# Every third weight remainder of three expert slots made by GpSimd instead of VectorE

## The chip, the cores and the metric

The kernel runs on one core of a Trainium2 chip. The core's engines run side by side, each through its own list of instructions in order: TensorE (PE in the profile; PEld is its loading of weights), VectorE (DVE), ScalarE (ACT), GpSimd (POOL) and SyncE (SP). Semaphores hold an instruction back until what it needs is done. The metric is the device time of one execution in microseconds; of several runs, the median.

## The reference

Attention comes first, then a layer of experts that takes the attention's output as its rows (3584 tokens of 768 values):

```python
q_n, k_n = (rmsnorm(q, g_q), rmsnorm(k, g_k))     # 8 batches, 12 heads, 448 positions, 64 values
scores = scale * np.matmul(q_n, k_n.transpose(0, 1, 3, 2))
attn = softmax(scores); x = attn @ v               # put together to x: 3584 x 768
logits = x @ w_gate + modality_bias[modality_id]   # 8 experts
e_idx = np.argmax(logits, axis=1)                  # one expert for each token
for e in range(8):
    h = np.maximum(x[mask] @ w1[e], 0.0)           # 768 -> 1024
    out[mask] = gate_w[mask, None] * (h @ w2[e])   # 1024 -> 768
```

All of it is in float32. The change touches only how `w1` is made ready for the product `x[mask] @ w1[e]`.

## The kernel before, in words

**Three products for one.** TensorE works here on a rounded 32-bit type (fp32r). To keep accuracy, a matrix is split into a rounded part and a remainder: `high = round(w)`, `low = w - high`. The product is then the sum of three, high times high, high times low and low times high. The first layer's weights are split by `split1`: ScalarE casts a piece of the raw weights `r1` into `w1h`, and VectorE subtracts it from the raw piece and writes the remainder to `w1l`. Both lie in the tile `w1w`. A piece is 128 partitions by 256 values; a slot needs 24 of them (4 groups `jj` of hidden values by 6 chunks `i` of the 768 inputs). The raw weights lie so that the 256 values of a piece are every eighth value of a row (`"p (c m j) -> p c j m"` with `j=8`), 32 bytes apart.

**Slots.** The tokens are sorted by expert into blocks of 256 rows, and a slot is one block. Fourteen slots run in a fixed loop (`for s in range(NSTAT)`), and what is left of the data goes through a tail behind it. A slot has two halves:

- the first layer (`mm1_half`, L485): eight beats, each 18 matmuls, two beats for each `jj`. The sums lie in two PSUM buffers `ph`, which ScalarE and VectorE empty into `hhw` and `hlw`; VectorE and ScalarE also split the second layer's weights here (`split2`, into `w2ha`/`w2hb` and `w2lw`);
- the second layer (`mm2_step`, L515): sixteen beats `b_`. Here the next slot is made ready: its rows are transposed after beats 9, 11 and 13 (`xtr`, L468, tile `px`), and split by ScalarE and VectorE into `xw`; and its 24 pieces of weights are split, two a beat in beats 0 to 11, by the loop `while s + 1 < NSTAT and k_ < ...`. The order of the pieces is chunks 0 to 2 of each of the four `jj`, then chunks 3 to 5 of each.

**The order is written out by hand.** `tc.manual_schedule` covers all five engines: every engine runs its instructions in the order in which the Python code issues them, and only the waits are added. So a place in the loop is a place in each engine's list. Most small operations go through the class `Deferred`, whose line 52 issues them at once (L52 in the profile) and whose line 53 issues those that were collected in a list and are dealt out later, five a beat (`little`).

**GpSimd's list.** In the slots before the change, GpSimd only issues indirect DMAs: `wload` (weights of a coming slot into `r`, which is `r1`, in beat 13, and into `r2w` during the first layer; a block of the same expert as the one before skips the rows but not the instruction), `xload` (rows of the slot after next into `xrw`, in beat 12, and for slot 3 at the start of slot 2; from slot 3 on two gathers for each half of the rows, the second of which waits for the first to land), the output scatter `out_dram<-yw` after each half of the second layer, `route_put` (`l_d<-lt`, the sorted token lists, in slots 0 and 1) and the gathers of the lists `lt<-l_d`. Six of the latter stand in slot 1 behind beat 10's pieces; VectorE works them up (`lb_x2f`, `lb_x2i`, `lb_oi`, `lb_o`) behind beat 15.

**Slots 0 and 1 differ from the others.** In slot 0, VectorE also finishes the routing of the last batch (`route_mm`, `route_pos`; tiles `rtc`, `bs`, `pf`), and in slot 1 it works out the tables of the remaining slots (`tables2`; tiles `tb_...`).

Of the kernel before, what the change touches and what calls it, by code (L numbers as in the profile page):

```python
# [9 lines left out]
F32 = mybir.dt.float32  # L10
# [3 lines left out]
ALU = mybir.AluOpType  # L14
# [43 lines left out]
def deferred(fn):  # L58

    Deferred.queue = items = []  # L60
    fn()
    Deferred.queue = None
    return items
# [3 lines left out]
def kernel(  # L67
# [15 lines left out]
    V, A, G = (Deferred(e, n) for e, n in ((nc.vector, "op"), (nc.scalar, "act"), (nc.gpsimd, "dma")))  # L83
    PE, SY = nc.tensor, nc.sync
    GP = Deferred(nc.gpsimd, "op")
# [16 lines left out]
        out=tri, in_=ones[:CP, :CP], pattern=[[1, CP]], compare_op=ALU.is_gt,  # L102
# [249 lines left out]
    def view(t, off, p, *dims):  # L352
        n = 1
        for d in dims:
            n *= d
        a = t[:p, off : off + n]
        if len(dims) > 1:
            ax = " ".join("abcd"[: len(dims)])
            a = a.rearrange(f"p ({ax}) -> p {ax}", **dict(zip("abcd"[1:], dims[1:])))
        return a  # L360
# [43 lines left out]
    w1h, w1l = ([view(w1w, 1536 * (2 * j + o), 128, 6, 2, 128) for j in range(4)] for o in range(2))  # L404
# [22 lines left out]
    def wload(s, which, halves=(0, 1)):  # L427
        tb, i = tb_of(s)
        raw, src = ((r1, w1v), (r2, w2v))[which]
        for h in halves:  # L430
            G.indirect_dma_start(out=raw[h], out_offset=None, in_=src,
                                 in_offset=IOFF(ap=tb["wi"][:, i, h : h + 1], axis=0),
                                 bounds_check=NE * 256 - 1, oob_is_err=False)

    def split1(jj, n0=0, n1=6):
        for i in range(n0, n1):
            h, c = divmod(i, 3)
            rs = r1[h].rearrange("p (c m j) -> p c j m", c=3, j=8)[:, c, 2 * jj : 2 * jj + 2]
            A.copy(w1h[jj][:, i], rs)
            V.tensor_tensor(out=w1l[jj][:, i], in0=rs, in1=w1h[jj][:, i].bitcast(F32), op=ALU.subtract)  # L440

    def split2(jj, only=None):
        rs = r2[jj // 2].rearrange("p (c f) -> p c f", c=4)[:, 2 * (jj % 2) : 2 * (jj % 2) + 2]
# [5 lines left out]
    def xload(s):  # L449
        tb, i = tb_of(s)  # L450
        xr = []
        for t in range(2):
            x = xr_b[s % 2][t]
            G.indirect_dma_start(out=x, out_offset=None, in_=x1_d[:],
                                 in_offset=IOFF(ap=lt2[:, s, t, 0:1].bitcast(I32), axis=0),
                                 bounds_check=NT1 - 1, oob_is_err=False)
            if tb["x2i"] is not None:
                G.indirect_dma_start(out=x, out_offset=None, in_=x2_d[:],
                                     in_offset=IOFF(ap=tb["x2i"][:, i, t : t + 1], axis=0),
                                     bounds_check=NT - NT1 - 1, oob_is_err=False)  # L460
            xr.append(x.rearrange("p (m c) -> p c m", c=6))
        return xr
# [14 lines left out]
    def mm1_open(s, jj):  # L477
        return ps_s.tile([128, 2, TB], F32, tag="s", name=f"ph{s}_{jj}")
# [27 lines left out]
    def mm2_open(s, t):  # L506
        pools = ((ps_t, "t"), (ps_t, "t")) if t == 0 else ((ps_m, "m"), (ps_o, "o"))
        return [p.tile([128, 512], F32, tag=tg, name=f"py{s}_{t}{n}") for n, (p, tg) in enumerate(pools)]
# [179 lines left out]
    if True:  # L688
# [354 lines left out]
        def route_mm(b, pool=(ps_t, "t")):  # L1043
            oh = RT[b]["oh"]
            ps = pool[0].tile([128, 512], F32, tag=pool[1], name=f"rt{b}")
            ohf = oh.rearrange("p c e -> p (c e)")
            PE.matmul(ps[:, 0:32], lhsT=ones[:CP, :128], rhs=ohf, start=True, stop=True)
            PE.matmul(ps[:CP, 32:64], lhsT=tri, rhs=ohf, start=True, stop=True)
            pc = rp.tile([128, 2, NCH, NE], F32, tag="rtc", name=f"rtc{b}")
            RT[b]["pc"] = pc  # L1050

            def evac():
                for i, r in ((0, slice(0, 128)), (1, slice(0, CP))):
                    V.tensor_copy(out=pc[r, i].rearrange("p c e -> p (c e)"), in_=ps[r, 32 * i : 32 * i + 32])

            return evac
# [32 lines left out]
        def route_put(b, c):  # L1089
            posi, lt = RT[b]["posi"], RT[b]["lt"]  # L1090
            G.indirect_dma_start(out=l_d[:], out_offset=IOFF(ap=posi[:, c : c + 1], axis=0),
                                 in_=lt[:, c, :], in_offset=None)
# [59 lines left out]
        def at(where, n, fn):  # L1152
            where.setdefault(n, []).append(fn)

        def run(where, n):
            for f in where.pop(n, ()):
                f()
# [29 lines left out]
        for u in range(NU):  # L1187
            for j in range(NJ):
                jj = (0, 1, 2, 4, 5, 6, 3)[j] if u < P["early"] else j
# [24 lines left out]
        for n in range(P["start"], NJ * NU):  # L1214
            i, j = divmod(n, NJ)
# [105 lines left out]
        def go(*fs):  # L1321

            for f in fs:
                r = f() or ()
                for g in after:
                    g()
                after[:] = r if isinstance(r, (list, tuple)) else [r]

        def part(fn, *a):
            return lambda: fn(*a)  # L1330
# [41 lines left out]
        def little(m):  # L1372
            for _ in range(min(m, len(small))):
                small.pop(0)[1]()

        for s in range(NSTAT):

            beat = {}
            if s > 0:
                if s == 1:  # L1380
                    xr = xn
                    for c in range(2):
                        at(beat, 3 * c, lambda c=c: route_put(B - 1, 2 + c))
                if s > 1:
                    xr = xn
                if s == 2:
                    xr = []
                    at(beat, 1, lambda: xr.extend(xload(3)))
                for b_ in range(4):
                    at(beat, 2 * b_, part(split2, b_))  # L1390
                    if b_ % 2:
                        at(beat, 2 * b_, part(wload, s + 1, 1, (b_ // 2,)))
                if s == 1:
                    small += deferred(tables2)
                elif s < NS2 - NS1:
                    for kind, fn in deferred(lambda: state["get2"](s + 1, 1 if s < NSTAT - 1 else NS2 - NSTAT)):
                        at(beat, 3 if kind == "dma" else 16, fn)
                for b_ in range(8):
                    if b_ % 2 == 0:
                        p0 = mm1_open(s, b_ // 2)  # L1400
                    go(part(mm1_half, s, b_ // 2, b_ % 2, p0))
                    run(beat, b_)
                    little(5)
            else:
                for c in range(NCH):
                    at(beat, 8 + 3 * c, lambda c=c: route_put(B - 2, c))
                    if c < 2:
                        at(beat, 20 + 3 * c, lambda c=c: route_put(B - 1, c))
            k_ = 0
            parts = [(b_, 3 * h + c) for h in range(2) for b_ in range(4) for c in range(3)]  # L1410
            for b_ in range(16):
                t, j = divmod(b_, 8)
                if j == 0:
                    p2 = mm2_open(s, t)
                go(part(mm2_step, s, t, p2, j))
                if j == 7:
                    go(part(mm2_done, s, t, p2))
                if s == 0 and b_ == 7:
                    route_mm(B - 1, (ps_a, "a"))()
                    small += deferred(lambda: route_pos(B - 1))  # L1420

                if s == NSTAT - 1:
                    if b_ == 0:
                        steps = small_slot(s + 1, xr)
                    for k in STEPS.get(b_, ()):
                        steps[k]()
                if b_ in XTB and s + 1 < NSTAT:
                    xtr(s + 1, xr, XTB.index(b_))()
                while s + 1 < NSTAT and k_ < min(24, (b_ - SP0 + 1) * SPN):
                    split1(parts[k_][0], parts[k_][1], parts[k_][1] + 1)  # L1430
                    k_ += 1
                little(5)
                run(beat, b_ + 8)
                if b_ == 12 and s != 1 and s + 2 <= NSTAT:
                    xn = xload(s + 2)
                if b_ == 13 and s + 2 <= NSTAT:
                    wload(s + 2, 0)
                if s == 1 and b_ == 9:
                    while small:
                        little(1)  # L1440
                    for kind, fn in deferred(lambda: state["get2"](0, 3)):
                        at(beat, 18 if kind == "dma" else 23, fn)
# [59 lines left out]
```

## Time and profile before

| | before |
|---|---|
| median of 3 runs | 1118.18 us (1115.25 to 1121.1) |
| the profiled execution | 1117.32 us |
| its span | 1115.6 us, mean granted TensorE clock 0.98 |
| busy, share of the span: PE / DVE / ACT / POOL | 96% / 76% / 72% / 59% |

The span begins with the first and ends with the last recorded instruction of the profiled execution. Attention takes up about the first 576 us; the first product of slot 0 starts at 576.1 us. Slot 0's second layer starts at 602.3 us, slot 1's first layer at 623.5 and its second at 641.6, slot 2's first at 661.2 and its second at 681.4, and slot 3's first at 699.6; from there a slot takes 35.5 us.

In the lines of the profile, `out<-in` names tiles without their numbers, `128x256` is partitions by elements, and `x24` is a count. In the grouped view, the numbers after the bar are the busy time of the group in us, the mean time of one in ns, and the idle time of the engine just before them with what ended it. In the timeline they are start and duration in us, and in brackets the idle time before. A timeline row of several instructions gives their common duration.

### The profile page before, as it was taken

How to read it: one execution, taken by the hardware profiler on the slowest of the kernel's cores; microseconds unless marked ns; L12 is line 12 of the kernel's file. 1: busy time of each engine (PE TensorE's matmuls, PEld its weight loads, DVE VectorE, ACT ScalarE, POOL GpSimd, SP SyncE). 2: the span in 40 equal slices, each digit the busy share in tenths (PEclk: the TensorE clock that was granted, in tenths of full speed). 3: DMA queues.
4: the chain of work that ended last, by engine and by line, in shares of the span. 5: the costliest groups of instructions: out<-in, count | busy, mean ns of one | idle time of the engine just before them, and what ended most of it. 6: DMA issues, size and time to landing. Idle time of an engine off the chain costs nothing.

```text
span 1115.6 us, 19940 instructions
## 1 busy us (share of the span) xinstructions
PE 1071.5 (96%) x6728; PEld 836.4 (75%) x6728; DVE 846.1 (76%) x1583; ACT 805.0 (72%) x1517; POOL 657.3 (59%) x658
## 2 busy tenths in 40 slices
PE   7899999999999999999999999999999999999993
PEld 6755655555555555655559899999999999999993
DVE  4677778988889988889698978767777787767730
ACT  4778888878888788776677677668866777667820
POOL 4377767788877788777864565354334423354251
PEclk6999999999999999999999999999999999999997
DMA  6757677677776788666824202111161111111170
GB/s 165 158 134 167 141 177 168 155 173 168 160 180 149 175 166 180 150 139 114 239 87 141 57 16 65 36 58 44 43 256 57 57 44 43 30 58 58 38 246 33
DMA packets 127967, 131.75 MB, mean 118 GB/s; under 512 B 68891, under 2 KB 122607, under 8 KB 126320
## 3 DMA queue, kind: packets, MB, share of 16 engines
q1 hardware_dynamic: 110212, 88.58, 34.9%
q0 software_dynamic: 17616, 41.80, 11.9%
q8 instruction: 55, 0.90, 0.4%
q14 instruction: 56, 0.46, 0.2%
q10 hardware_dynamic: 28, 0.01, 0.0%
HBM read 148.74 MB, written 22.38 MB: 153 GB/s over the span
## 4 chain that ended last, share of the span: by engine, by line
PE 75%; DVE 12%; DMA 5%; issue 3%; ACT 2%; SPq 1%; POOL 1%; ACTq 0%; POOLq 0%; DVEq 0%
PE ph L485 18%; PE py L515 16%; PE av L936 13%; PE st L897 12%; PE sa L869 5%; PE tr L792 3%; DVE at_hlw L52 3%; DVE w1w L52 2%; PE xt L993 2%; DMA lt<-l_d,tb_li 2%; PE px L468 2%; PE sm L951 2%; DMA w1w<-xw 1%; DVE xw L52 1%; PE sm L958 1%
## 5 line engine op out<-in xcount | busy, mean ns | idle before, releaser
L485 PE MATMUL ph<-xw,w1w 128*128 128x256 f32 x2016 | 246.1, 284 | 3.0 <-DVE hlw L52 2.3
L485 PEld LDWEIGHTS ph<-xw,w1w 128*128 128x128 f32 x2016 | 243.9, 192 | 5.1 <-DVE hlw L52 2.5
L52 DVE TENSOR_REDUCE at_hlw<-sa 128x1 f32<-128x448 f32 x336 | 206.5, 617 | 45.2 <-PE sa L869 27.4
L52 DVE TENSOR_TENSOR w1w<-r,w1w 128x256 fp32r<-128x256 f32 x336 | 206.8, 673 | 12.5 <-ACT w1w L52 12.5
L52 ACT CAST w1w<-r 128x256 fp32r<-128x256 f32 x336 | 210.2, 726 | 0.0
L897 PE MATMUL st<-w1w 128*128 128x448 f32 (+1 forms) x480 | 176.4, 417 | 1.6 <-ACT r2w L52 1.6
L52 ACT ACTIVATE r2w<-st 128x448 f32<-128x448 f32 x168 | 90.9, 543 | 50.0 <-PE st L897 42.8
L52 ACT ACTIVATE hhw<-ph 128x512 fp32r<-128x512 f32 x56 | 33.5, 598 | 123.1 <-PE ph L485 123.1
L869 PE MATMUL sa<-w1w 128*128 128x448 f32 (+1 forms) x288 | 110.6, 385 | 11.6 <-DVE at_hlw L52 5.8
L897 PEld LDWEIGHTS st<-w1w 128*128 128x128 f32 (+1 forms) x480 | 85.0, 191 | 44.1 <-ACT r2w L52 20.4
L52 POOL TENSOR_TENSOR r2w<-r2w 128x448 f32<-128x448 f32 (+1 forms) x72 | 83.0, 1152 | 56.1 <-DVE r2w L52 21.3
L515 PE MATMUL py<-w2lw,hhw 128*128 128x384 f32 x448 | 113.8, 335 | 0.0
L52 ACT CAST w1w<-xw 64x448 fp32r<-64x448 f32 x188 | 105.3, 561 | 2.0
L52 ACT ACTIVATE at_w2lw<-st 128x448 f32<-128x448 f32 x168 | 90.9, 544 | 21.6 <-PE st L897 15.8
L897 PE MATMUL st<-w1w,w2ha 65*128 65x448 f32 x288 | 100.6, 369 | 1.3 <-DMA w1w<-xw 1.3
L52 POOL DMA_INDIRECT out_dram<-yw,lb_oi x22 | 26.1, 1187 | 121.4 <-ACT yw L52 116.0
L52 POOL TENSOR_TENSOR xrw<-r,at_hlw 112x512 f32<-112x512 f32 x94 | 96.7, 1047 | 0.6 <-PE tr L792 0.3
L515 PEld LDWEIGHTS py<-w2lw,hhw 128*128 128x128 f32 x448 | 80.9, 188 | 0.0
L52 DVE SCALAR_TENSOR_TENSOR hlw<-ph,hhw 128x512 fp32r<-128x512 f32 x56 | 38.7, 690 | 52.0 <-ACT hhw L52 51.9
L52 POOL TENSOR_TENSOR r2w<-r2w,at_w2lw 64x448 f32<-64x448 f32 (+1 forms) x48 | 55.6, 1159 | 30.8 <-DVE r2w L52 14.6
L869 PEld LDWEIGHTS sa<-w1w 128*128 128x128 f32 (+1 forms) x288 | 55.5, 193 | 24.2 <-DVE at_hlw L52 9.0
L52 POOL DMA_INDIRECT xrw<-x_d,lb_x2i x24 | 29.5, 1230 | 67.2 <-DMA xrw<-x_d,lt 63.6
(301 smaller groups left out, 2278.4 us busy)
## 6 DMA issues: line engine op xcount, KB each, us to landing
w1w<-xw SPq DMA_DIRECT2D x312, 112.0 KB
r<-in_q_dram SPq DMA_DIRECT2D x48, 224.0 KB
r<-in_k_dram SPq DMA_DIRECT2D x48, 224.0 KB
w2ha<-xw SPq DMA_DIRECT2D x72, 112.0 KB
x_d<-at_w2hb SPq DMA_DIRECT2D x8, 672.0 KB
x_d<-yw SPq DMA_DIRECT2D x8, 672.0 KB
r2w<-in_v_dram SPq DMA_DIRECT2D x48, 96.0 KB
at_w2lw<-in_v_dram SPq DMA_DIRECT2D x48, 96.0 KB
```

Of the source, the lines that this page charges most:

```text
L52: return fn(*a, **kw)
L468: PE.transpose(ps[:, i, 128 * t : 128 * t + 128], xr[t][:, 2 * g + i], idn)
L485: PE.matmul(ps[:, i], lhsT=lt_, rhs=rt_[:, c], start=n == 0, stop=n == 17)
L515: PE.matmul(ps[n][:, :384], lhsT=lt_[:, j, 128 * t : 128 * t + 128], rhs=rt_[:, 384 * n : 384 * n + 384], start=j == 0 and m == 0, stop=j ...
L792: PE.transpose(sp[:, c], src[:, c], idn[:CP, :CP])
L869: PE.matmul(ps[:, :S], lhsT=t["qq"][r, h, a : a + 128], rhs=t["kk"][h][r], start=True, stop=True)
L897: PE.matmul(ps[:, :S], lhsT=l, rhs=t["qq"][:, h] if first else t["ql"][:, h], start=first and (j != 3 or h == 0), stop=not first and (j != ...
L936: PE.matmul(t["av"][64 * h : 64 * h + 64, :S], lhsT=vv[r, u % 3, j], rhs=t["p"][r, j], start=c == 0, stop=c == 3)
L951: PE.matmul(R[g][32 * i : 32 * i + 32, :S], lhsT=sel[:, m], rhs=T[u + i // 2]["cs"][:, i % 2], start=m == 0, stop=False, tile_position=(0, ...
L958: PE.matmul(sm[32 * i : 32 * i + 32, :S], lhsT=wg[:, (4 * g + i) % NP], rhs=T[4 * g + i]["xt"], start=False, stop=True, tile_position=(0, ...
L993: PE.transpose(ps[:CP, 128 * c : 128 * c + 128], T[u]["xt"][:, c * CP : (c + 1) * CP], idn)
```

## The change

`split1` gets an argument `low`, the engine that subtracts. In the loop that makes ready the next slot's first layer, slots 0, 1 and 2 hand GpSimd (`GP`) the remainder of every third piece: steps 2, 5, 8, 11, 14, 17, 20 and 23 of 24, eight a slot, in beats 1, 2, 4, 5, 7, 8, 10 and 11. These are chunks 2 and 5 of each `jj`. The casts stay with ScalarE, and all other slots and `split1` calls stay with VectorE. (`GP` and the object `G` that issues GpSimd's DMAs are the same engine and the same list.)

```diff
-    def split1(jj, n0=0, n1=6):
+    def split1(jj, n0=0, n1=6, low=V):
         for i in range(n0, n1):
             h, c = divmod(i, 3)
             rs = r1[h].rearrange("p (c m j) -> p c j m", c=3, j=8)[:, c, 2 * jj : 2 * jj + 2]
             A.copy(w1h[jj][:, i], rs)
-            V.tensor_tensor(out=w1l[jj][:, i], in0=rs, in1=w1h[jj][:, i].bitcast(F32), op=ALU.subtract)
+            low.tensor_tensor(out=w1l[jj][:, i], in0=rs, in1=w1h[jj][:, i].bitcast(F32), op=ALU.subtract)
...
                 while s + 1 < NSTAT and k_ < min(24, (b_ - SP0 + 1) * SPN):
-                    split1(parts[k_][0], parts[k_][1], parts[k_][1] + 1)
+
+                    split1(parts[k_][0], parts[k_][1], parts[k_][1] + 1,
+                           GP if s < 3 and k_ % 3 == 2 else V)
                     k_ += 1
```

## The prediction

> **What bounds the kernel now.** I read the page first, then the waits of TensorE over the first slots, then the chain of waits through them, then the timelines of GpSimd, VectorE and ScalarE there.
>
> The page's span, and the group that the change splits (count, busy us, mean ns of one):
>
> ```profile
> span 1115.6 us, 19940 instructions
> L52 DVE TENSOR_TENSOR w1w<-r,w1w 128x256 fp32r<-128x256 f32 x336 | 206.8, 673 | 12.5 <-ACT w1w L52 12.5
> ```
>
> 336 remainders are 14 slots of 24; 24 of them move. The waits of TensorE between 602 and 683 us, where slots 0 and 1 and the start of slot 2 lie (us in total, times, longest):
>
> ```profile
> PE px L468 <- DVE xw L52: 2.5, 2, 1.5
> PE ph L485 <- DVE hlw L52: 2.3, 1, 2.3
> PE ph L485 <- DVE xw L52: 0.6, 1, 0.6
> PE px L468 <- DVE rtc L52: 0.4, 1, 0.4
> ```
>
> Together 5.8 us: that is all that a quicker VectorE could win. 5.6 us is 0.5% of the time, about the least that a measurement of this kernel tells from no change; so a gain that can be told from none is nearly shut out before any costing. The chain of waits shows which of these stalls decides:
>
> ```profile
> 658.40 0.54 DVE w1w L52
> 658.94 3.86 DMA lt<-l_d,tb_li
> ...
> 667.19 2.37 DMA lt<-l_d,tb_li
> ...
> 671.88 0.69 DVE hlw L52
> ...
> 672.62 8.90 PE ph L485 x72
> ...
> 699.76 17.27 PE ph L485 x144
> ```
>
> TensorE's restart at 672.62 does not hang on the remainders but on six small gathers (lt) that GpSimd issues at the end of slot 1; VectorE waits for their last landing and only then frees a PSUM buffer (hlw). Whatever slots 0 and 1 win earlier is lost in that 2.3 us wait unless the gathers come earlier too. From 672.62 the chain is TensorE's own work, so slots 2 and 3 have nothing to win, only to lose. GpSimd's timeline there (start, us, then in brackets the idle time before):
>
> ```profile
> 648.96 1.03 POOL L52 DMA_INDIRECT r2w<-in_moe_w_dram,ta_wi  x1 [0.30 <-DVE tb_ch L53]
> 653.24 5.40 POOL L52 DMA_INDIRECT out_dram<-yw,la_oi  x1 [3.25 <-ACT yw L52]
> 658.94 2.49 POOL L53 DMA_INDIRECT lt<-l_d,tb_li  x1 [0.30 <-DVE w1w L52]
> 661.73 1.40 POOL L53 DMA_INDIRECT lt<-l_d,tb_li  x1 [0.30 <-issue]
> ...
> 667.19 0.95 POOL L53 DMA_INDIRECT lt<-l_d,tb_li  x1 [0.30 <-issue]
> ...
> 691.25 1.00 POOL L52 DMA_INDIRECT r2w<-in_moe_w_dram,tb_wi  x1 [0.30 <-issue]
> ...
> 694.47 1.12 POOL L52 DMA_INDIRECT xrw<-x_d,lt  x1 [0.30 <-issue]
> ...
> 705.90 1.00 POOL L52 DMA_INDIRECT r<-in_moe_w_dram,tb_wi  x1 [0.30 <-issue]
> ```
>
> An issue takes about 1 us, but one took 5.40. VectorE's timeline beside it, and GpSimd and VectorE at an earlier case of the same:
>
> ```profile
> 652.14 5.66 DVE L52 TENSOR_TENSOR w1w<-r,w1w 128x256 fp32r<-128x256 f32 x10
> 657.73 0.67 DVE L52 TENSOR_TENSOR xw<-px,xw 128x512 fp32r<-128x512 f32 x1
> 596.67 3.42 DVE L52 TENSOR_TENSOR w2lw<-r2w,w2ha 128x1536 fp32r<-128x1536 f32 x2
> 597.60 3.36 POOL L52 DMA_INDIRECT r<-in_moe_w_dram,ta_wi  x1 [0.30 <-issue]
> ```
>
> Both issues end 0.85 to 0.9 us after a run of VectorE instructions with two SBUF inputs ends (657.8 to 658.64, 600.09 to 600.96): while such a run lasts, an issue can stand still. A remainder costs VectorE 0.57 us (5.66/10).
>
> **The change part by part.** VectorE loses 8 instructions of 0.57 us, 4.5 us, in each of slots 0, 1 and 2. ScalarE's casts, TensorE's matmuls and SP's queue keep theirs. GpSimd gains 8 instructions a slot: steps 2, 5, 8, 11, 14, 17, 20 and 23 of 24. They sit in program order before the output scatter (the first five), before the six gathers (17 and 20) and before the row and weight gathers of a later slot (23 too), and each waits for its cast on ScalarE with all of these behind it.
>
> Their price is not in the trace. The nearest GpSimd rows, and two pairs that show what reading every eighth element costs elsewhere:
>
> ```profile
> L52 POOL TENSOR_TENSOR r2w<-r2w 128x448 f32<-128x448 f32 x48 | 55.2, 1150 | 40.6 <-DVE r2w L52 21.3 <-ACT at_w2lw L52 18.1 <-DVE rsm L53 0.8
> L53 POOL TENSOR_TENSOR at_hlw<-at_hlw 112x48 f32<-112x48 f32 x42 | 12.8, 304 | 5.3 <-ACT at_hlw L53 4.0
> L52 ACT CAST w1w<-r 128x256 fp32r<-128x256 f32 x336 | 210.2, 726 | 0.0
> L52 ACT CAST xw<-px 128x512 fp32r<-128x512 f32 x42 | 26.8, 639 | 1.5 <-PE px L468 1.5
> L52 DVE TENSOR_TENSOR xw<-px,xw 128x512 fp32r<-128x512 f32 x42 | 28.9, 687 | 0.0
> ```
>
> A line through 304 ns at 48 elements and 1150 at 448 (2.1 ns an element over 0.2 us) gives 0.74 us for 256: the lower end. On ScalarE and VectorE the strided 256 cost as much as 512 in order, so a doubled element is the upper end: 0.2 + 1.08 = 1.29 us. I take 1.0, the middle. [...]
>
> Then the two engines get in each other's way. Two windows of the grouped view, VectorE's remainders in 555 to 582 us (GpSimd adding tensors) and in 602 to 662 us (GpSimd only issuing DMAs), and single rows of both engines:
>
> ```profile
> L52 DVE TENSOR_TENSOR w1w<-r,w1w 128x256 fp32r<-128x256 f32 x12 | 11.5, 969 | 0.7 <-ACT w1w L52 0.7
> L52 DVE TENSOR_TENSOR w1w<-r,w1w 128x256 fp32r<-128x256 f32 x48 | 28.2, 653 | 0.0
> 558.38 1.14 POOL L52 TENSOR_TENSOR at_hhw<-r2w,at_w2lw 128x448 f32<-128x448 f32 x1
> 558.70 1.25 DVE L52 TENSOR_TENSOR w1w<-r,w1w 128x256 fp32r<-128x256 f32 x1 [0.51 <-ACT w1w L52]
> 559.48 1.43 POOL L52 TENSOR_TENSOR r2w<-r2w 128x448 f32<-128x448 f32 x1
> 570.11 1.45 POOL L52 TENSOR_TENSOR r2w<-at_w2lw 128x448 f32<-128x448 f32 x1
> 570.53 0.67 DVE L52 TENSOR_TENSOR xw<-px,xw 128x512 fp32r<-128x512 f32 x1
> ```
>
> A remainder that meets a GpSimd addition waits until that has read (1.25), the next addition waits for the remainder (1.43 for 1.14), and an instruction with one operand in PSUM runs through (0.67). So each moved remainder gives VectorE 0.57 us and costs another remainder 0.32 us (969 - 653) on average, and where both engines have a queue, the whole reading time. [...] On GpSimd I count 1.2 us a step: 1.0, half of 1.43 - 1.14, and 0.05 between instructions.
>
> Term a, the gathers of slot 1. The queue is free for step 2 at 648.96 + 1.03 + 0.3 = 650.3; five steps end at 656.3. Of VectorE's ten remainders six stay: 6 x 0.57 + 5 x 0.32 = 5.0, to 657.1; the scatter ends 0.85 later at 658.0 (now 658.64); steps 17 and 20 and a gap of 0.3 bring the first gather to 660.7, 1.8 later than 658.94. By then VectorE's run is over, and the first two gathers need 0.95 each and not 2.49 and 1.40: 2.0 back. **a = -0.2.** The cover is 3.25 us of idle time, 4.4 of the scatter's excess and those 2.0; without it, seven steps would be 8.4 us late. Bounds: at 0.8 a step (0.74 and a gap) and no excess, the scatter runs 654.3 to 655.3, step 20 is done at 657.0, so -1.9 - 2.0 = -3.9; at 1.29 + 0.57 = 1.86 a step, 659.6 after five, 664.6 after seven, +5.7 - 2.0 = +3.7. Slot 0's own stalls (under 2.6 us) cost or win nothing, as the wait at 672.62 takes them up.
>
> Term b, the end of slot 2. GpSimd reaches step 2 only behind slot 1's step 23 and the gather of 691.25, at 693.6. So its steps fall where VectorE has five remainders and the last transposed rows to finish:
>
> ```profile
> 699.75 0.77 DVE L52 TENSOR_TENSOR xw<-px,xw 128x512 fp32r<-128x512 f32 x1
> 717.56 9.86 ACT L52 CAST w1w<-r 128x256 fp32r<-128x256 f32 x16
> ```
>
> Now these rows end near 700.4 and are read at the thirteenth matmul after 699.76, at 701.2 (17.27/144 = 0.12 each). Three remainders less (-1.7), five waits of 0.32 to 0.75 more (+1.6 to +3.8): 0 to 1.3 late. **b = +0.3.**
>
> Term c, slot 3. Eight steps and a scatter (1.3) from 693.6 end at 704.5, so the row gathers start 10 us later than 694.47, and the weight gather not at 705.90 but at 715.9. Landing times of that tile in slots 0 to 2:
>
> ```profile
> DMA to landing us min/median/max: 2.1/2.9/6.2
> ```
>
> It lands at 718.8, and ScalarE wants it at 717.56, in the stretch where it casts without a pause; so what is late there passes on to the end of slot 3. **c = +1.2**, from 0 (eight steps of 0.8: 712) to 5.4 (1.86 a step: 722.0 and 2.9, against 719.5 after a 1.9 us stall of the same kind in b). ScalarE has no slack there: each further us of GpSimd's backlog costs one.
>
> Sum against the profiled execution's 1117.32: -0.2 + 0.3 + 1.2 = 1118.6. The median of the runs shown, 1118.18, lies 0.9 above that execution; **1119.5**.
>
> **The rivals.**
>
> First, the relief wins. GpSimd's step costs 0.8 us, the engines rarely meet, and the scatter no longer stands behind a run of ten: a = -3.9, b = c = 0, 1113.4 and by the median 1114.3. For it speaks that VectorE's run is broken up; against it that the meeting is in the trace, at 969 ns.
>
> Second, slower: GpSimd's queue decides. If a step with its wait is 1.86 us, a = +3.7, step 14 of slot 2 comes at 703.7 where slot 3's first group needs it at 701.8 (b = +1.9), c = +5.4: 1128.3, by the median 1129.2. It decides from about 1.5 us a step, where the sum passes +5.6. For it: strided reads doubled on two engines. Against: additions of 448 elements among VectorE's took 1.45.
>
> Third, the issue's standing still is not VectorE's doing. Then neither the 4.4 nor the 2.0 us come back, a = 7 x 1.2 - 3.25 = +5.2, with b and c 1124.0, by the median 1124.9. Against it: the 0.85 us in both places. [...]
>
> **How the numbers follow.** Forecast 0.57, relief 0.22, queue 0.15, third 0.06. The forecast's own range is 1116 to 1123. Relief reaches 1114.3 and seldom passes 1112.6 (0.5% below): faster 0.04. Slower (over 1123.8): two thirds of the queue's 0.15, half of the third, and a little of the forecast: 0.16. Same: 0.80. For 8 in 10 I take 1114 to 1126: relief's time below, part of the queue's above.
>
> **What would show it.** In the changed profile: 24 GpSimd TENSOR_TENSOR w1w at 0.9 to 1.3 us (over 1.5: the second rival; under 0.8: the first); VectorE's remainders in slots 0 to 2 at a higher mean than 653 ns; the first of the six gathers at 660 to 661.5, and TensorE's restart within 1 us of 672.6; the scatter of slot 1 well under 5.40 (at 5.40 still: the third); a wait of ScalarE's casts for the weight gather in slot 3 of 1 to 3 us. I am wrong if TensorE's stalls of 5.8 us are mostly gone, or if GpSimd's queue is late by more than 5 us at slot 2.

## The result and the profile after

The changed kernel took 1129.32 us (median of six runs, 1127.91 to 1136.76) against 1117.21 for the kernel before (six runs, 1115.25 to 1121.1), a ratio of 1.0102 [1.007, 1.0134]: slower by 1.0%. The forecast was 1119.5 us, with 1114 to 1126.

The two lines of the changed kernel's page that answer to those of before:

```profile
span 1135.0 us, 19959 instructions
L52 DVE TENSOR_TENSOR w1w<-r,w1w 128x256 fp32r<-128x256 f32 x312 | 203.3, 708 | 15.3 <-ACT w1w L52 14.4
```

VectorE has lost its 24 instructions but only 3.5 us of busy time (206.8 before), since the mean of the rest rose from 673 to 708 ns. In this profiled execution the attention part took some 10 us longer (slot 0's first product starts at 586.42 us and not at 576.11). The change doesn't touch that part, and the later profiles of other kernels start anywhere from 573.9 to 581.1; so stages are compared by their offset from that first product:

| offset, us | slot 1 begins | slot 2 | slot 3 | last product of slot 13 |
|---|---|---|---|---|
| before | 47.4 | 85.1 | 123.5 | 521.0 |
| after | 54.0 | 91.0 | 133.0 | 530.5 |

By these offsets the loss is 9.5 us, it is complete when slot 3 begins, and it arises in two places: 6.6 us in slot 0 and some 6 in slot 2's second layer, with about 3 gained between. The ratio stands for 11.4 us (7.8 to 15.0), the difference of the medians for 12.1; what goes beyond the 9.5 lies outside these stages and is not explained. TensorE's waits over slots 0 to 3 of the changed kernel (576 to 800 us; one that belongs to the attention's end is left out; total, times, longest):

```profile
PE px L468 <- DVE xw L52: 10.3, 3, 4.7
PE px L468 <- DVE rtc L52: 1.7, 1, 1.7
...
PE ph L485 <- DVE hlw L52: 0.2, 1, 0.2
```

Together 12.2 us against 5.8 before. Nearly all of it is one thing: the transposes of the next slot's rows (`px`) wait for VectorE to empty a PSUM buffer into `xw`. The price of the new instructions, and VectorE's remainders beside them, from the grouped view of 600 to 735 us:

```profile
L52 DVE TENSOR_TENSOR w1w<-r,w1w 128x256 fp32r<-128x256 f32 x51 | 40.9, 842 | 3.6 <-ACT w1w L52 2.6 <-ACT yw L52 0.9
L52 POOL TENSOR_TENSOR w1w<-r,w1w 128x256 fp32r<-128x256 f32 x24 | 22.6, 956 | 5.3 <-ACT w1w L52 5.1
```

GpSimd's step costs 0.956 us; that was foreseen (1.0). Why VectorE is late is in the timelines of both engines, here slot 0 and then slot 2:

```profile
619.49 1.08 POOL L52 DMA_INDIRECT l_d<-lt,posi  x1 [0.31 <-issue]
620.60 1.78 POOL L52 TENSOR_TENSOR w1w<-r,w1w 128x256 fp32r<-128x256 f32 x2
620.28 2.54 DVE L52 TENSOR_TENSOR w1w<-r,w1w 128x256 fp32r<-128x256 f32 x1
633.05 2.11 DVE L53 CAST posi<-pos 112x4 int32<-112x4 f32 x1
...
707.22 4.40 POOL L52 TENSOR_TENSOR w1w<-r,w1w 128x256 fp32r<-128x256 f32 x5
707.23 4.78 DVE L52 TENSOR_TENSOR w1w<-r,w1w 128x256 fp32r<-128x256 f32 x1 [0.94 <-ACT yw L52]
```

GpSimd's five steps run without a gap, 0.88 us each, and one VectorE instruction of some 0.6 us takes 4.78: it gets its turn only when the whole run is over. Two steps in a row hold a remainder for 2.54, and two more a cast of 4 columns for 2.11. All that stands behind on VectorE is late by as much, the `xw` of the next transposes with it.

The waits then cost more than their length. TensorE's timeline after the two longest:

```profile
635.80 1.14 PE L468 MATMUL px<-idn,xrw 128*128 128x128 f32 x4 [4.67 <-DVE xw L52]
637.38 0.84 PE L515 MATMUL py<-w2lw,hhw 128*128 128x384 f32 x2
640.38 17.43 PE L485 MATMUL ph<-xw,w1w 128*128 128x256 f32 x144
715.31 1.15 PE L468 MATMUL px<-idn,xrw 128*128 128x128 f32 x4 [4.34 <-DVE xw L52]
719.43 2.79 PE L485 MATMUL ph<-xw,w1w 128*128 128x256 f32 x22
```

and the same stretch of the kernel before, behind its wait of 1.52 us:

```profile
620.74 0.81 PE L468 MATMUL px<-idn,xrw 128*128 128x128 f32 x4 [1.52 <-DVE xw L52]
621.74 0.51 PE L515 MATMUL py<-w2lw,hhw 128*128 128x384 f32 x2
623.48 1.71 PE L485 MATMUL ph<-xw,w1w 128*128 128x256 f32 x13
```

From the transposes to the next slot it is 2.74 us before, and 4.58 and 4.12 after: 1.8 and 1.4 us of slower clock. The windowed view of the changed kernel gives the granted clock of these stretches (the first of the last three numbers) as 0.83 and 0.91 (1.00 in all others from 600 to 740 us):

```profile
620.00:640.00 20.00, 13.60 (x71) 12.96 (x71) 19.32 (x33) 12.89 (x24) 13.90 (x15) 0.83 0.06 20
700.00:720.00 20.00, 15.66 (x87) 15.35 (x86) 15.69 (x20) 13.34 (x25) 15.00 (x16) 0.91 0.13 40
```

The sum: waits 12.2 - 5.8 = 6.4, clock 1.8 + 1.4 = 3.2, together 9.6 beside the 9.5 of the offsets.

### The profile page after: what moved, and what is told of

Same layout as the page of the kernel before. It is cut to its first block, busy times and chain, and to the rows that moved or that the text cites. A ratio compares the mean times of both kernels' runs of the same rounds, so it can differ in the third digit from the quotient of the medians.

```text
span 1135.0 us, 19959 instructions
## 1 busy us (share of the span) xinstructions
PE 1078.3 (95%) x6728; PEld 837.5 (74%) x6728; DVE 858.5 (76%) x1559; ACT 805.8 (71%) x1517; POOL 672.0 (59%) x682
## 4 chain that ended last, share of the span: by engine, by line
PE 70%; DVE 12%; DMA 6%; issue 4%; POOL 2%; ACT 2%; SPq 1%; ACTq 0%; POOLq 0%; DVEq 0%
PE ph L485 18%; PE py L515 16%; PE av L936 11%; PE st L897 11%; PE sa L869 4%; DVE at_hlw L52 3%; PE tr L792 2%; DVE w1w L52 2%; DMA w1w<-xw 2%; PE xt L993 2%; PE px L468 2%; PE sm L951 1%; DVE xw L52 1%; DMA lt<-l_d,tb_li 1%; POOL r2w L52 1%
## 5 line engine op out<-in xcount | busy, mean ns | idle before, releaser
L52 DVE TENSOR_TENSOR w1w<-r,w1w 128x256 fp32r<-128x256 f32 x312 | 203.3, 708 | 15.3 <-ACT w1w L52 14.4
L52 DVE TENSOR_TENSOR w2lw<-r2w,w2ha 128x1536 fp32r<-128x1536 f32 x28 | 49.2, 1760 | 30.9 <-ACT w2ha L52 22.5
```

The source lines that it names most:

```text
L52: return fn(*a, **kw)
```

## The experiments

Two theories stood at first. **Port:** a run of GpSimd's steps holds VectorE up (4.78 us for one instruction above), so the loss lies where the steps stand, in the waits for `xw`. The port is the author's picture of what one engine holds against the other; no run shows it. **Queue:** GpSimd's list is too long, so what it issues comes late. The stage offsets of all timed kernels, with the ratio to the kernel before:

| kernel | slot 1 | slot 2 | slot 3 | last | ratio [95%] |
|---|---|---|---|---|---|
| slot 0 only | 54.0 | 90.6 | 126.6 | 524.1 | 1.0058 [1.0035, 1.0081] |
| slot 1 only | 47.4 | 90.2 | 125.9 | 523.4 | 1.0026 [1.0009, 1.0043] |
| slot 2 only | 47.3 | 85.0 | 128.4 | 526.4 | 1.0084 [1.0056, 1.0112] |
| copy of VectorE's piece ahead | 47.6 | 85.9 | 133.3 | 530.9 | 1.0076 [1.0052, 1.0099] |
| two fills ahead of each step | 46.9 | 83.4 | 129.6 | 532.0 | 1.0113 [1.0074, 1.0152] |
| fills, no steps | 47.4 | 85.6 | 125.5 | 523.4 | 1.0 [0.9974, 1.0026] |
| copy of GpSimd's own piece ahead | 49.3 | 90.1 | 126.0 | 524.0 | 1.0022 [1.0003, 1.0042] |

Before is 47.4, 85.1, 123.5, 521.0. An offset near 2 us by itself proves little: the fills' +2.4 goes with a ratio of 1.0. For slot 0 alone and slot 2 alone the ratios stand for 6.5 and 9.4 us, some 3 and 4 more than the offsets' 3.1 and 5.4; as above, that rest is not explained. Three more kernels (the price, where a run begins, dependent or not) had one execution each, 1120.57, 1128.56 and 1116.8 us, and are read for their rows alone.

### Each slot alone

```diff
-                           GP if s < 3 and k_ % 3 == 2 else V)
+                           GP if s == 0 and k_ % 3 == 2 else V)
```

and the same with 1 and with 2.

> Only slot 0 keeps the changed steps. Port theory (two or more GpSimd subtractions that stand next to each other in its list, both ready, hold the port without letting VectorE in between): VectorE instructions of 2 to 2.6 us beside each pair, TensorE waits in slot 0 about 7 us instead of 2.5, and some of it is taken up by the 2.3 us wait of slot 2's first layer, so +3 to +5 us over before. Queue theory (what is late is GpSimd's own list): in slot 0 the list has idle time between the list writes, so at most +1 us.

> Only slot 1 keeps the changed steps. Port theory: here each step waits for its cast and stands alone, so no VectorE instruction waits over 1.4 us, the output scatter is no longer stretched to 5.4 us and the six gathers come no later: 0 to -3 us against before. Queue theory: seven steps ahead of the six gathers make these late, TensorE's wait before slot 2's second half grows from 2.3 us, +2 us or more.

> Only slot 2 keeps the changed steps. Port theory: the first five steps pile up behind the weight gather of the first layer and run without a gap, one VectorE remainder waits over 4 us, TensorE waits over 4 us for the last transposed rows and then runs at a lower clock for 2 to 3 us: +5 to +6 us. Queue theory: the cost lies in slot 3, where ScalarE's casts wait for the weight gather; TensorE waits at most 1 us at the end of slot 2 and 1 to 3 us at the end of slot 3.

Slot 0 alone costs 6.6 us there. Slot 2 takes up 2.4 of them, by the wait that the prediction named, and slot 1 takes up 1.1, where TensorE's own waits for `xw` get shorter; 3.1 stay. Slot 2 alone costs 5.0 there and 5.4 at the end. So the port theory's places are right and the queue theory's (later gathers, a wait in slot 3) are not. The two add up to 8.5 of the 9.5 us.

Slot 1 alone was to cost nothing, by the port theory too, as its steps stand singly in the changed kernel, each waiting for its cast (5.1 us of idle time in the group's row above). Here it lost 5.1 us in slot 1, and 2.4 by the end. GpSimd came to its first step 7.6 us after ScalarE's casts had begun, so the five steps' casts were done or came in time; in the changed kernel it came 2.0 us after that, and waited for each. There slot 0's loss had made the casts late (they begin at an offset of 71.9 us, here at 66.4), and GpSimd not. So the steps of slot 1 stood singly only because slot 0 had lost time. GpSimd, VectorE and TensorE there:

```profile
653.85 4.51 POOL L52 TENSOR_TENSOR w1w<-r,w1w 128x256 fp32r<-128x256 f32 x5
653.35 5.03 DVE L53 TENSOR_TENSOR lf<-lf 1x1 f32<-1x1 f32 x1
665.28 1.15 PE L468 MATMUL px<-idn,xrw 128*128 128x128 f32 x4 [3.91 <-DVE xw L52]
```

An instruction on a single element is held for 5.03 us (the like took 0.15 in the kernel before). The six gathers came no later than before (the first at 82.5 us for 82.8), so what was lost here is VectorE's time and not the list's. So it is not the number of steps in a slot that costs, but whether they pile up; that part of the expectation was wrong. The same pair of rows for slot 2 alone:

```profile
693.13 4.41 POOL L52 TENSOR_TENSOR w1w<-r,w1w 128x256 fp32r<-128x256 f32 x5
693.46 4.52 DVE L52 TENSOR_TENSOR w1w<-r,w1w 128x256 fp32r<-128x256 f32 x1 [0.58 <-ACT w1w L52]
```

### Making GpSimd take turns

Ahead of each step a one-column copy reads the piece that VectorE made in the step before, so that GpSimd has to wait for VectorE:

```diff
+                    if s < 3 and k_ % 3 == 2:
+                        jp, ip = parts[k_ - 1]
+                        GP.tensor_copy(out=seen, in_=w1l[jp][:, ip, 0, 0:1].bitcast(F32))
```

> All 24 steps stay on GpSimd, but ahead of each GpSimd copies one column of the step before it, which VectorE makes; so no two subtractions stand next to each other and VectorE comes in between. Port theory: no VectorE remainder waits over 1.5 us, TensorE's longest wait in slots 0 to 2 is under 2.5 us, and the time is within 3 us of before. Queue theory: GpSimd's list gets longer and waits more than in the change, so the time is that of the change (+12 us) or more.

Mixed. Slots 0 and 1 are back at 47.6 and 85.9: the loss there vanished with the piling. But slot 2 lost 9 us all the same (47.4 from start to start, 38.4 before). There GpSimd arrives so late that VectorE's pieces are long made, and the copies, which have nothing to wait for, neither hold it nor let VectorE in:

```profile
698.15 0.20 POOL L52 COPY seen<-w1w 128x1 f32<-128x1 f32 x1
698.30 0.93 POOL L52 TENSOR_TENSOR w1w<-r,w1w 128x256 fp32r<-128x256 f32 x1
...
698.12 5.42 DVE L52 TENSOR_TENSOR w1w<-r,w1w 128x256 fp32r<-128x256 f32 x1 [0.98 <-ACT w1w L52]
675.81 4.38 PE L485 MATMUL ph<-xw,w1w 128*128 128x256 f32 x22 [4.17 <-DVE hlw L52]
```

The wait of 4.17 us for `hlw` (2.27 before) is the queue theory's: the longer list makes slot 1's gathers later. With both costs the offset at the end is no better than the changed kernel's (530.9 and 530.5), and the expectation of a time within 3 us of before failed.

### The price in quiet slots

VectorE keeps all its work; in beat 3 of six later slots GpSimd gets five more instructions. They write the same values again or a scratch tile, so no result changes. The edit, shortened: slots 5 and 7 subtract as the change does (7 the same piece five times), 9 puts a waiting copy ahead of each, 10 only copies (one input), 11 subtracts into one scratch tile with its input in order, 12 only fills.

```diff
+            if s == 10:
+                GP.tensor_copy(out=scr, in_=w1h[jj][:, i].bitcast(F32))
+            elif s == 12:
+                GP.memset(scr, 0.0)
+            else:
+                GP.tensor_tensor(out=o, in0=rs, in1=w1h[jj][:, i].bitcast(F32), op=ALU.subtract)
```

> VectorE makes all remainders as before; in the quiet slots 5, 7, 9, 10, 11 and 12 GpSimd gets five extra instructions in beat 3, while VectorE runs through its sixteen remainders. Slot 5: five subtractions of different pieces again; slot 7: five times the same piece; slot 9: five pieces with a one-column copy of a VectorE piece ahead of each; slot 10: five one-input copies of 256 elements to one scratch tile; slot 11: five subtractions with 256 elements in order to the scratch tile; slot 12: five fills of the scratch tile. Port theory: in slot 5 one VectorE remainder lasts 4 to 5 us, in slots 7 and 9, where a subtraction has to wait for something, none over 1.6 us, and in slot 12 none over 0.8 us. Rival (turns, as the prediction had it: each waiting instruction gets the port after one of the other engine): 0.9 to 1.6 us in all of slots 5 to 11. Price: 0.85 to 0.95 us a strided subtraction, 0.7 to 0.8 with elements in order.

GpSimd's rows and VectorE's beside them, for slots 5 and 10, and VectorE's for slot 12:

```profile
790.64 6.15 POOL L52 TENSOR_TENSOR w1w<-r,w1w 128x256 fp32r<-128x256 f32 x5 [1.34 <-DVE w1w L52]
789.82 13.58 DVE L52 TENSOR_TENSOR w1w<-r,w1w 128x256 fp32r<-128x256 f32 x18
...
970.93 3.44 POOL L52 COPY scr<-w1w 128x256 f32<-128x256 f32 x5 [0.52 <-ACT w1w L52]
970.93 9.81 DVE L52 TENSOR_TENSOR w1w<-r,w1w 128x256 fp32r<-128x256 f32 x16
...
1041.95 9.74 DVE L52 TENSOR_TENSOR w1w<-r,w1w 128x256 fp32r<-128x256 f32 x16
```

Copies and fills cost VectorE nothing (9.81 and 9.74 us for 16, 0.61 each; 9.69 to 9.81 in the kernel before). The subtractions do, but in another way than in the changed kernel: five take 6.15 us, 1.23 each, and VectorE's 18 take 13.58 where 18 times 0.61 would be 11.0. Here the engines do alternate, at 0.5 us lost for each step, in the way that the prediction had assumed (0.32 to 0.75). The expectation for slot 5, one instruction of 4 to 5 us, failed, though its five steps depend on none of each other, as in the change; unlike there, each writes a piece that VectorE has written before. So the same instruction alternates in one place and shuts VectorE out in another, and what decides was open.

### Single steps

In slot 0 only, and only steps 2, 8, 14 and 20, each of which then stands alone between two DMA issues:

```diff
+                           GP if s == 0 and k_ in (2, 8, 14, 20) else V)
```

> Only slot 0, and there only steps 2, 8, 14 and 20, so that every subtraction stands alone between two DMA issues. Port theory: no VectorE instruction over 1.8 us, slot 1's first layer starts 47 to 48.5 us after slot 0's (47.4 before, 54.0 with eight steps). If the cost goes by the number of steps: half of 6.6 us, 50.7.

Slot 1 began at 48.8 (+1.4), and the last product at 520.6 (-0.4): 1119.22 us beside 1118.9 on the same chip, one run each. Half of the steps cost a fifth of the 6.6, so it is not their number.

### Where a run begins

First guess: a run that stands directly behind a DMA's issue keeps VectorE out, as all runs that did so in the profiles so far begin 0.01 to 0.03 us behind one (620.60 behind 619.49 + 1.08 above).

```diff
+            for _ in range({5: 0, 7: 1}.get(s, 5)):
+                GP.memset(scr, 0.0)
+            if s in (10, 11, 12):
+                G.indirect_dma_start(out=lt3, out_offset=None, in_=l_d[:],
+                                     in_offset=IOFF(ap=tb["li"][:, i, 0:1], axis=0))
+            if s == 11:
+                GP.memset(scr, 0.0)
+            for _ in range(5):
+                GP.tensor_tensor(out=scr, in0=r1[0]..., in1=scr, op=ALU.subtract)
```

> VectorE's work is that of the kernel before; GpSimd gets five subtractions of the same strided 128x256 form in six quiet slots, into a scratch tile that nobody reads, so no result changes. Only where the run begins differs. Slot 5: directly behind the weight gather's issue, before VectorE's run of remainders. Slot 7: one fill of 128x256 (0.36 us) lies between. Slot 9: five fills lie between, so that the run begins in the middle of VectorE's run. Slots 10 and 12: five fills, then one more list gather's issue, then the run directly behind it, in the middle of VectorE's run. Slot 11: as 10, with one fill between the issue and the run. What is open: in the changed kernel's slots 0 and 2 the run kept VectorE out (one instruction of 4.78 us), in the earlier price run five such subtractions alternated with VectorE at 1.23 us each. Theory 'the run behind an issue keeps the port': slots 10 and 12 show five subtractions at 0.85 to 0.95 us and one VectorE instruction of 4 to 5 us; slots 9 and 11 show 1.15 to 1.3 us each and no VectorE instruction over 1.5 us; slot 5 keeps VectorE out once for 3 to 5 us, slot 7 as slot 5 if being first is enough, or as slot 9 if the issue is what counts. Rival 'steps of the changed kernel differ in their waits or their tiles': all six slots alternate.

All six slots alternate, also slot 5, where the run stands directly behind the issue (five in 5.89 us, 1.18 each):

```profile
791.12 1.01 POOL L52 DMA_INDIRECT r2w<-in_moe_w_dram,tb_wi  x1 [2.48 <-DVE w2lw L52]
792.16 5.89 POOL L52 TENSOR_TENSOR scr<-r,scr 128x256 f32<-128x256 f32 x5
```

Standing behind an issue is not enough. But these five subtractions all read and write one tile, so each depends on the one ahead of it; the 24 steps of the change depend on none of each other.

### Dependent or not, first or not

Five subtractions of 128x192, in slots 5, 9 and 11 into two scratch tiles in turn, in slots 7 and 12 into one:

```diff
+            if s == 9:
+                for _ in range(6):
+                    GP.memset(scr[0], 0.0)
...
+                GP.tensor_tensor(out=scr[n % 2 if s in (5, 9, 11) else 0], in0=rv[:, 0, 0:2, 0:96], in1=two,
+                                 op=ALU.subtract)
```

> VectorE's work is that of the kernel before; GpSimd gets five subtractions of 128x192 into scratch tiles that nobody reads, behind the weight gather's issue of five quiet slots, so no result changes. Slots 5, 9 and 11: into two scratch tiles in turn, so that a subtraction depends on none just ahead of it (slot 9 behind six fills, in the middle of VectorE's run; slot 11 with the cast piece as second input, as in the changed kernel). Slots 7 and 12: all into one scratch tile, so that each writes what the one ahead of it wrote (slot 12 with the cast piece as input). Theory 'independence': GpSimd starts a subtraction that depends on none just ahead of it before that one's end, and the port is not let go in between; so in slots 5, 9 and 11 one VectorE instruction takes 3 us or more while five subtractions go at about 0.7 us each, and in slots 7 and 12 the two engines take turns, at 1.0 to 1.3 us a subtraction and with no VectorE instruction over 1.5 us. Rival 'something else of the changed kernel's slots': all five slots alternate. If slot 9 alone alternates among the independent ones, being first counts too.

Rows of GpSimd and VectorE in slots 5, 7, 9 and 11:

```profile
785.09 4.23 POOL L52 TENSOR_TENSOR scr<-r 128x192 f32<-128x192 f32 x5
785.58 4.18 DVE L52 TENSOR_TENSOR w1w<-r,w1w 128x256 fp32r<-128x256 f32 x1
...
858.69 5.42 POOL L52 TENSOR_TENSOR scr<-r 128x192 f32<-128x192 f32 x5
859.20 12.63 DVE L52 TENSOR_TENSOR w1w<-r,w1w 128x256 fp32r<-128x256 f32 x18
...
931.85 5.70 POOL L52 TENSOR_TENSOR scr<-r 128x192 f32<-128x192 f32 x5
930.43 13.20 DVE L52 TENSOR_TENSOR w1w<-r,w1w 128x256 fp32r<-128x256 f32 x18
...
1002.20 5.34 POOL L52 TENSOR_TENSOR scr<-r,w1w 128x192 f32<-128x192 f32 x5 [0.55 <-ACT w1w L52]
1002.18 12.48 DVE L52 TENSOR_TENSOR w1w<-r,w1w 128x256 fp32r<-128x256 f32 x18
```

In slot 5 GpSimd is first (785.09 against VectorE's 785.58) and its steps are independent: the five take 0.85 us each, and VectorE stands for 4.18. In slot 7 GpSimd is first as well, but each step depends on the last: they alternate. That pair shows that independence is needed. In slots 9 and 11 the steps are independent, but VectorE's run of remainders had begun 1.4 and 0.02 us before them: they alternate, so independence is not enough. The expectation had slots 9 and 11 held by independence alone; that being first counts too it allowed only for slot 9. Slot 12, dependent and with VectorE first, alternates as expected (five in 5.36 us).

What the second condition is stays open. Being first by the records is not it: in slot 1 alone the instruction held for 5.03 us began 0.5 us before GpSimd's run (653.35 and 653.85), and in the changed kernel's slot 0 the one of 2.54 us began 0.32 us before (620.28 and 620.60), in the middle of a run of ten remainders that had begun at 618.52. What these two have in common with every run that kept VectorE out is the place: such a run begins 0.00 to 0.03 us behind the issue of an indirect DMA (in the kernel with turns, its first copy does). In those two cases VectorE's instruction began while that issue was still going on. Slot 5 here stands 0.03 us behind one too; slots 9 and 11, and slot 5 of the run on the price, don't (fills, or a wait of 0.55 or 1.34 us, lie between). So a rival fits all these records: a run of independent steps keeps VectorE out if it stands directly behind an issue, whichever engine began first. It was not tested: only dependent steps were tried with nothing but the place changed.

### The same in the kernel itself

Three kernels put the two costs apart. The fills alone, at the places of the steps, with VectorE making all remainders, and the changed kernel with two fills ahead of each step:

```diff
+                    if s < 3 and k_ % 3 == 2:
+                        GP.memset(scr, 0.0)
+                        GP.memset(scr, 0.0)
```

> VectorE makes all remainders, as before; at the 24 places of the change GpSimd's list gets two fills of a 128x320 scratch tile (about 0.45 us each, so about as long as a step, with no input); no result changes. Port theory: no VectorE instruction is held, slots 0 and 2 as before, the end within 2 us of before (the list gathers of slot 1 may come a little later). Queue theory: the loss is GpSimd's time, so the end is +6 to +12 as in the changed kernel.

> The changed kernel with two fills of a 128x256 scratch tile (0.36 us each) on GpSimd ahead of each of its 24 steps; no result changes. Port theory (what costs the time is that a gapless run keeps VectorE out): the steps alternate with VectorE's, no VectorE instruction over 2 us in slots 0 and 2, slot 0 within +1.5 us of before, slot 2 at most +2.5, the end within +4 of before, though GpSimd's list is longer by 24 times 0.72 us. If fills let VectorE in no better than the one-column copies did: slot 0 near +0, slot 2 again near +6, the end near +9. Queue theory (GpSimd's list itself is what is too long): worse than the changed kernel, +12 or more.

The fills alone (128x320 here) lengthen GpSimd's list by 24 times two fills of 371 ns, 17.8 us, and the time shows no cost (1.0 [0.9974, 1.0026]). The change's steps are 22.6 us, and unlike the fills they wait for casts, so this alone doesn't clear the list; but in the changed kernel the signs of a late list are missing as well (TensorE's wait for `hlw` is 0.2 us, and ScalarE's casts in slot 3 wait for no weights). With fills and steps VectorE gets in between (slots 1 and 2 begin at 46.9 and 83.4, a little earlier than before), but now the list is what costs, with (29.2 + 15.3) / 24 = 1.9 us a step. The groups of GpSimd in that kernel from 600 to 760 us:

```profile
L52 POOL TENSOR_TENSOR w1w<-r,w1w 128x256 fp32r<-128x256 f32 x24 | 29.2, 1217 | 0.0
L52 POOL MEMSET scr<- 128x256 f32 x48 | 15.3, 320 | 1.4
```

The waits of TensorE from 600 to 800 us:

```profile
PE ph L485 <- DVE hlw L52: 8.1, 1, 8.1
```

And ScalarE's timeline in slot 3:

```profile
729.50 9.76 ACT L52 CAST w1w<-r 128x256 fp32r<-128x256 f32 x16 [4.14 <-DMA r<-in_moe_w_dram,tb_wi]
```

8.1 us for the list gathers and 4.14 for slot 3's weights: one theory's cost was traded for the other's. The port theory's expectation, the end within 4 us of before, failed: it came 11.0 us later, near the queue theory's 12 or more.

Last, the changed kernel with a one-column copy out of the piece that GpSimd's *own* last step made, so that each step depends on the one ahead and the list grows by little:

```diff
+                    if s < 3 and k_ % 3 == 2 and k_ > 2:
+                        jp, ip = parts[k_ - 3]
+                        GP.tensor_copy(out=seen, in_=w1l[jp][:, ip, 0, 0:1].bitcast(F32))
```

> The changed kernel with a one-column copy on GpSimd ahead of each of its steps but the first of a slot, out of the piece that GpSimd's own last step made (about 0.2 us; in the earlier run of turns the copy read VectorE's piece, which was often long done); no result changes. Independence theory: the copy has to wait for the end of GpSimd's step, so the run breaks up and VectorE gets in between; no VectorE instruction over 2 us in slots 0 and 2, slot 2's length within 2.5 us of before, the end at +2 to +5 (the list gathers of slot 1 some 2 us later). If the port is kept through such a copy too: slot 2 again near +6 and the end near +9.5. Queue theory: no better than the changed kernel.

GpSimd and VectorE at the start of slot 2's run, where the changed kernel had 4.78:

```profile
690.13 1.04 POOL L52 TENSOR_TENSOR w1w<-r,w1w 128x256 fp32r<-128x256 f32 x1
691.60 1.30 POOL L52 TENSOR_TENSOR w1w<-r,w1w 128x256 fp32r<-128x256 f32 x1
690.36 1.29 DVE L52 TENSOR_TENSOR w1w<-r,w1w 128x256 fp32r<-128x256 f32 x1 [0.59 <-DMA lt<-l_d,tb_li]
```

VectorE waits for one step and not for five. With copies at the same places that had nothing to wait for, it had been held for 5.42 us; so it is the dependence, and not the copies, that lets VectorE in. Slot 2 shows no wait for `xw` over 0.2 us, and it takes 35.9 us from start to start (42.0 in the changed kernel). The ratio is 1.0022 [1.0003, 1.0042] where the changed kernel has 1.0102: by the ratios four fifths of the loss is gone, by the offsets two thirds (3.0 of 9.5 us stay), with 21 small copies added. Slots 0 and 1 lose 5.0 us, and slot 2 takes up 2.5 of them; that was not followed further. No kernel here beat the one before by more than a measurement can tell.

## Why the prediction was wrong

**What bounds the kernel** was read rightly: there were 5.8 us to win at most, and they lay in VectorE's waits.

**The price** was right (1.0 against 0.956 us), and with it the second rival's condition failed: a step did not reach 1.5 us. That rival's 1129.2 us is close to the time, but for another reason. Its mechanism is real all the same: at 1.9 us a step, in the kernel with fills, the gathers and slot 3's weights came late as it says, and the time was 1130.13.

**The step that failed** is the way the two engines meet: "A remainder that meets a GpSimd addition waits until that has read", 0.32 us on average. The rows that it came from were of GpSimd additions in the attention part, one or two beside a VectorE instruction, and there the engines did alternate (1.25 us for VectorE's, 1.43 for GpSimd's next). From this term b took "five waits of 0.32 to 0.75", +0.3 us with at most 1.3. Measured: one wait of 4.34 us, and 1.4 more for the clock. The row of the five steps that stand ready in a queue was in the working ("GpSimd reaches step 2 only behind slot 1's step 23 and the gather of 691.25"); what was missing was the question what five ready instructions in a row do to the other engine.

**"Slot 0's own stalls (under 2.6 us) cost or win nothing, as the wait at 672.62 takes them up"** failed in its size. The mechanism was right: that wait fell from 2.27 to 0.21 us. But slot 0 lost 6.6 us and the cover holds 2.3 (3.5 with the 1.1 us by which slot 1 itself got shorter, by the run of slot 0 alone). The prediction looked only at what slot 0 could win; a run of two steps there, 2.54 us, was not costed.

**Term a** (-0.2) came near by luck: slot 1 took 37.0 us from start to start and not 37.7. That was so only because slot 0 had lost 6.6 us, which the prediction put at nothing, and the steps of slot 1 then waited for their casts one by one. With slot 0 as it was, as the term assumes, slot 1 lost 5.1 us (slot 1 alone): the gathers came no later than worked out, but VectorE was shut out there too. The scatter's row shows that the relief came as worked out, and the third rival, by which it would stay at 5.40, falls. The signs named for the first gather and for TensorE's restart did not come, since slot 0's loss moved both (first gather at an offset of 87.4 for 82.8, restart at 100.0 for 96.5):

```profile
669.28 1.02 POOL L52 DMA_INDIRECT out_dram<-yw,la_oi  x1 [0.42 <-ACT yw L52]
673.77 1.07 POOL L53 DMA_INDIRECT lt<-l_d,tb_li  x1
686.44 3.74 PE L485 MATMUL ph<-xw,w1w 128*128 128x256 f32 x29 [0.21 <-DVE hlw L52]
737.39 9.88 ACT L52 CAST w1w<-r 128x256 fp32r<-128x256 f32 x16
```

**Term c** (+1.2) was 0: the last row has no wait. TensorE was late by then too, and with it the need for the weights. In the kernel with fills the same term was 4.14 us.

**The chances.** The 0.16 for slower rested mostly on the price of a step. No case had GpSimd's price as forecast and VectorE shut out.

## What to carry to other kernels

Work given to GpSimd beside a busy VectorE has to be priced by how it queues, not only by its duration: here five that stood ready in a row and didn't depend on one another kept VectorE out to the end of their run (4.78 us for one instruction), and TensorE's transposes behind it waited 4.34 us. Every such run stood directly behind the issue of an indirect DMA (0.00 to 0.03 us). Where such work must be moved, place single instructions between others (four lone steps in slot 0 put slot 1 back by 1.4 us, where eight had put it back by 6.6), or make each depend on the one ahead of it (1.29 us for VectorE's instruction at the start of slot 2's run), and look which wait of TensorE stands behind VectorE at that place. Taking turns has its price too: about 0.5 us of VectorE's time for each step here. Before calling a stall covered, compare the size of the cover with the whole run of instructions, and count the clock that TensorE loses after the wait (1.8 and 1.4 us here).

## What the runs showed of the hardware

- **Who is kept out.** Runs of independent GpSimd subtractions directly behind the issue of an indirect DMA kept VectorE out to their end (4.78, 5.42, 5.03, 4.52, 4.18 us for one instruction). With each step dependent on the one ahead, or away from such an issue with VectorE's run of remainders already going on, the engines alternated at 1.07 to 1.23 us a subtraction. What the two engines exclude each other from, why VectorE gets no turn between the five, and whether the DMA's issue ahead is needed, was not shown.
- **What is held.** Also a one-element instruction (5.03 us) and a cast of four columns (2.11) were held. Five one-input copies of GpSimd (`scr<-w1w`) held nothing (3.44 us for the five; 9.81 for VectorE's 16 remainders beside them, 9.69 to 9.81 in the kernel before).
- **TensorE's clock.** After waits of 4.67 and 4.34 us a pair of products took 0.84 us for 0.51 (granted clock 0.50 from 636 to 640 us and 0.67 from 716 to 720; 0.83 and 0.91 on average over the 20 us around them). In the last kernel, in slot 1, a wait of 2.27 us did the same (1.15 for 0.81, then 0.84 for 0.51, at a granted clock of 0.92 from 660 to 680 us), and a wait of 2.27 us in the kernel before did not (1.00 from 660 to 680). So the length of the wait alone does not decide; what else does was not shown. The last kernel's row:

```profile
659.77 1.15 PE L468 MATMUL px<-idn,xrw 128*128 128x128 f32 x4 [2.27 <-DVE xw L52]
```
